# Gradient of x in column strips for 12 of 16 row tiles: where its turns go on SyncE's queue, and five smaller moves

## The chip, the cores and the metric

The kernel runs on one core of one Trainium2 chip. The metric is the device time of one execution in microseconds (us); "the time" is the median over runs. An engine is named as in the profile: PE is TensorE's matmuls, PEld its weight loads, DVE is VectorE, ACT is ScalarE, POOL is GpSimd, SP is SyncE, which here only issues transfers.

## The reference

Forward and backward pass of one block, 2,048 rows (S) by 640 columns (D), in bf16. Only what matters here:

```python
h  = x + attn(layernorm(x), wqkv, wo)          # linear attention, 32 heads of 20
h2 = h + silu(hn @ w1) * (hn @ w3) @ w2        # hn = layernorm(h), F = 1728
# outputs: h2, and by vjp the gradients of x, wqkv, wo, w1, w3, w2
```

The gradient of x ends as: gxn = gq @ Wq.T + gk @ Wk.T + gv' @ W', a contraction over 15 blocks of 128 (five each of q, k and the third, whose rows the kernel keeps as `pkT` with a folded weight). Then the backward layernorm of each row of gxn (two sums over the row, then scale and shift), then the addition of the gradient that comes around the block.

## The kernel before

The rows are 16 tiles of 128 (ST = 16), also seen as 4 chunks of 512 (SC = 4, TPC = 4 tiles each); D is 5 blocks of 128 (DT = 5). Instructions stand on each engine in the order in which the program issues them, by hand; no scheduler moves them. `dma` and `dmaT` (copy, and copy with transposition) go to SP's queue, `dmaG` to POOL's.

The stages follow each other in time: projections and the linear attention (0 to 97 us), the gated MLP forward with half of its backward (97 to 340), gradient of w2 (340 to 398), gradient of hn and of the attention output (398 to 543), then the part that the change touches:

- **Fifth stage** (560 to 611 us): gradients of the q part of wqkv (`wq_jobs((0,))`), the 25 "squares" (L1378), and g_kT, the k gradient in column form (L1439 matmuls, L1445 on DVE). Squares put their result into slots of the ring `obs` (L1452), from where POOL's queue stores it (L1455). `bd`, which served as `gkvT` until then, is free behind that.
- **gxn stage** (611 to 676 us, loop at L1504 and after): `e_gxn(t)` makes the 128 rows of tile t: two halves of 320 columns, 15 matmuls each (L1495), the stationary operand being a 128x128 piece of the turned gradient, the moving one `wqT` with 320 columns. The q piece comes from `e_T(t)` (L1425), which turns g_q's tile t into a slot of `bd`, five tiles ahead. `ln_bwd` follows: ACT takes the row sum while it empties PSUM (L1143), DVE makes the second sum and the combination (L1146 to L1151), ACT scales (L1155), DVE adds (L1156), and SP stores the tile (`out1S`, L1513).
- **Turns of g_k** (`k_turn`, L1487): 20 transfers that bring g_kT back to rows, two per tile, for the k jobs that come next.
- **k jobs** (676 to 698 us): ten weight-gradient jobs of 16 matmuls of 320 columns (L1344), each emptied by ACT (L1348) and stored by SP (L1350). `njob` PSUM banks go round.
- **Last stage** (698 to 815 us): gradients of w1 and w3, 35 jobs of 16 matmuls of 496 columns, with `hnN` (normalised rows of h, loaded over g_q in four parts, L1483) stationary and `gb` blocks (turned from DRAM, L1475) moving. Block 0 of `gb` is loaded in three parts during the last gxn tiles.

Earlier, in the first 97 us, `r_head(t)` scales tile t of the attention's q side and turns it (`r_T`, L385); `r_store` (L735) stores it on POOL's queue. [...]

Of the kernel before, what the change touches and what calls it, by code (L numbers as in the profile page):

```python
# [9 lines left out]
P = 128  # L10
# [45 lines left out]
def kernel(  # L56
# [246 lines left out]
    def phi_rest(keep=0):  # L303
        while len(held) > keep:
            held.pop(0)()
# [78 lines left out]
    def r_T(t):  # L384
        dmaT(out=pqT[:, :, t * P:(t + 1) * P], in_=pqs[t])  # L385
# [47 lines left out]
    def m_end(m, js=(0, 1)):  # L433
        mb = mbs[:, m % 4, :]
        acc = macc[m]
        for j in js:
            A.copy(out=mb[:, j * HD:(j + 1) * HD], in_=acc[j][:, 0:HD])
        if m < 2:
            A.copy(out=Z[:, m:m + 1], in_=acc[1][:, HD:HD + 1])
            z_diag(m)  # L440
        if m < DT - 1:
            dmaT(out=mT[:, :, m * P:(m + 1) * P], in_=mb)
# [134 lines left out]
    def r_row(t):  # L577
        r_red(t)
        r_inv(t)
        r_scale(t)  # L580

    def r_head(t):
        r_row(t)
        r_T(t)
# [24 lines left out]
    phi_rest()  # L609
    m_part(3, range(5))  # L610
    q_tile(6)
    r_head(1)
    r_prod(3)
    phi_rest()
    m_part(3, range(5, 11))
# [4 lines left out]
    phi_rest()  # L620
    m_part(3, range(11, ST))
    m_end(3)
    r_T(2)
    load_w2T(4 * P, 8 * P)
    dmaG(out=m_v[:, 1:4, :], in_=mbs[:, 1:4, :])
# [4 lines left out]
    kvT_block(1, big())  # L630
    r_row(4)
    r_prod(6)
    phi_rest()
    m_part(4, range(5, 11))
    q_tile(9)
# [308 lines left out]
    def kv3():  # L944
# [5 lines left out]
        (f2_wT, 4), (phi_rest,), (q_late, 14), (r_T, 4), (r_head, 5), (load_x, 4, 6), (r_prod, 7),  # L950
        (q_out, 10, 14), (mlp_ghh, 4),
        (q_late, 15), (w2_room,), (sig_table,), (f2_half, 0, 0), (f2_half, 1, 0), (f2_half, 2, 0), (f2_half, 3, 0), (mlp_ghh, 5),
        (f2_half, 0, 1), (r_store, 4, 5), (f2_half, 1, 1), (f2_hn, 0), (r_store, 5, 6), (f2_half, 2, 1), (f2_hn, 1),
        (f2_half, 3, 1), (f2_m_out,),
        (f2_half, 4, 0, True), (mlp_ghh, 6), (f2_half, 4, 1, True), (f2_half, 5, 0, True), (r_red, 6, (0,)), (f2_hn, 2), (f2_hn, 3),
        (f2_ht, 2), (f2_ht, 3), (load_w2T, 8 * P, 10 * P), (mlp_ghh, 7), (r_red, 6, (1,)), (r_inv, 6), (r_scale, 6),
        (r_T, 6), (f2_rest,), (r_red, 7), (r_inv, 7), (r_scale, 7), (r_T, 7), (r_store, 6, 7))
# [177 lines left out]
                    yield  # L1135
        b_ln(acc, t)

    def ln_bwd(acc, t, nrm, st, out, res, pl, gs=None, y=None):

        if gs is None:  # L1140
            gs = pl.tile([P, D], BF16, name="gs", bufs=2)
        s = pl.tile([P, 4], F32, name="s", bufs=2)
        A.activation(out=gs[:].rearrange("p (j n) -> p j n", j=2), in_=acc[:, :, 0:HD], func=AF.Identity,  # L1143
                     accum_out=s[:, 0:1])
        wb = pl.tile([P, D], F32, name="wb", bufs=2)
        V.scalar_tensor_tensor(out=wb[:], in0=gs[:], scalar=1.0, in1=nrm, op0=ALU.mult, op1=ALU.mult,  # L1146
                               accum_out=s[:, 1:2])
        V.tensor_scalar(out=s[:, 2:3], in0=s[:, 1:2], scalar1=-1.0 / D, scalar2=None, op0=ALU.mult)
        V.tensor_scalar(out=s[:, 3:4], in0=s[:, 0:1], scalar1=-1.0 / D, scalar2=st.rs[:, t:t + 1],
                        op0=ALU.mult, op1=ALU.mult)  # L1150
        V.scalar_tensor_tensor(out=wb[:], in0=nrm, scalar=s[:, 2:3], in1=gs[:], op0=ALU.mult, op1=ALU.add)  # L1151

        def rest():
            yt = pl.tile([P, D], BF16, name="y") if y is None else y
            A.activation(out=yt[:], in_=wb[:], func=AF.Identity, bias=s[:, 3:4], scale=st.rs[:, t:t + 1])  # L1155
            V.tensor_tensor(out=out, in0=yt[:], in1=res, op=ALU.add)  # L1156
        return rest
# [176 lines left out]
    def grad_job(lhs, m, rhs, n, out, q=dma):  # L1334
        for _ in grad_halves(lhs, m, rhs, n, out, q):
            pass

    def grad_halves(lhs, m, rhs, n, out, q=dma):

        acc = ps.tile([P, 512], F32, name="job", bufs=njob)  # L1340
        for t in range(ST):
            if t == ST // 2:
                yield
            T.matmul(acc[:, 0:n], lhsT=lhs[:, t, m * P:(m + 1) * P], rhs=rhs(t), start=(t == 0),  # L1344
                     stop=(t == ST - 1))
        ob = obs[:, cnt[0] % (OB // n) * n:(cnt[0] % (OB // n) + 1) * n]
        cnt[0] += 1
        A.copy(out=ob, in_=acc[:, 0:n])  # L1348
        for x, y, to in out:
            q(out=to, in_=ob[:, x:y])  # L1350

    def half(src, j):
        return lambda t: src[:, t, j * HD:(j + 1) * HD]
# [3 lines left out]
    def wq_jobs(ks):  # L1357
        for m in range(DT):
            for k in ks:
                for j in range(2):  # L1360
                    yield from grad_halves(xnN, m, half(gqkv[k], j), HD,
                                           [(0, HD, out2S[:, m, k * D + j * HD:k * D + (j + 1) * HD])],
                                           dma if k else dmaG)
                    yield
# [55 lines left out]

    gT = {}

    def e_T(t):
        gT[t] = bd[:, t % DT, :].rearrange("p (k q) -> p k q", q=P)
        dmaT(out=gT[t], in_=g_q[:, t, :])  # L1425

    mN = U1.tile([P, DT, D], BF16, name="mN", tag="W6")
    load_pkT(2)
# [5 lines left out]
    for n in range(0, SC * DT, 2):  # L1434
        pair = [divmod(i, DT) for i in (n, n + 1)]
        acc = d_acc()
        for b, (c, d) in enumerate(pair):
            for k in range(DT):
                T.matmul(acc[:, b, :], lhsT=gm[:, k, d * P:(d + 1) * P], rhs=xnT[c][:, k, :], start=(k == 0),  # L1439
                         stop=(k == DT - 1))  # L1440
        for b, (c, d) in enumerate(pair):
            cs = slice(c * W, (c + 1) * W)
            pm = dx.tile([P, W], BF16, name="pm", bufs=2)
            V.tensor_scalar(out=pm[:], in0=pkT[:, d, cs], scalar1=1.0, scalar2=None, op0=ALU.min)
            V.scalar_tensor_tensor(out=g_kT[:, d, cs], in0=acc[:, b, :], scalar=gz[:, d:d + 1], in1=pm[:], op0=ALU.add,  # L1445
                                   op1=ALU.mult)
        if n < 16:
            fill(1)
        if 8 <= n < 8 + 2 * DT:
            i = n // 2 - 4  # L1450
            sq = square(mN, gkv_b, i)
            k = (4, 0, 1, 2, 3)[i]  # L1452
            ob = obs[:, k * D:(k + 1) * D]
            unload(sq, ob)
            dmaG(out=out2S[:, i, 2 * D:3 * D], in_=ob)  # L1455
    for t in range(DT):
        e_T(t)
    for _ in jobs:
        pass
    dx.release()  # L1460
    ba.release()


    ex = pool("ex", "right")
    hnN = g_q
    blocks = [(f0, min(f0 + NB, 2 * F)) for f0 in range(0, 2 * F, NB)]
    NB0 = 160

# [11 lines left out]
                for lo, out in ((0, out4S), (F, out5S)) if max(f0, lo) < min(f1, lo + F)]  # L1480

    def load_hnN(i):
        dma(out=hnN[:, i * TPC:(i + 1) * TPC, :], in_=hn_v[:, i * TPC:(i + 1) * TPC, :])  # L1483

    def k_turn(n):
        c, d = divmod(n, DT)
        dmaT(out=g_k[:, c * TPC:(c + 1) * TPC, d * P:(d + 1) * P], in_=g_kT[:, d, c * W:(c + 1) * W])  # L1487

    def e_gxn(t):
        acc = ps.tile([P, 2, 512], F32, name="gxn", tag="gxn", bufs=2)  # L1490
        for j in range(2):
            for k in range(15):
                ts = slice(t * P, (t + 1) * P)
                g = gT[t][:, k, :] if k < DT else g_kT[:, k - DT, ts] if k < 2 * DT else pkT[:, k - 2 * DT, ts]
                T.matmul(acc[:, j, 0:HD], lhsT=g, rhs=wqT[:, k, j * HD:(j + 1) * HD], start=(k == 0),  # L1495
                         stop=(k == 14))
        gx = scr[:, t % 2, :]
        ln_bwd(acc, t, xnN[:, t, :], ln1, gx, g_h[:, t, :], ex, scr[:, 2 + t % 2, :], scr[:, 4, :])()
        return gx

    ps.release()
    ps = pool("pep", space=PSUM)
    njob = 2
    jobs = wq_jobs((1,))  # L1504
    scr = U1.tile([P, DT, D], BF16, name="scr", tag="W6")
    for t in range(ST):
        gx = e_gxn(t)
        if t + DT < ST:
            e_T(t + DT)
        for n in (2 * t, 2 * t + 1):  # L1510
            if n < SC * DT:
                k_turn(n)
        dma(out=out1S[:, t, :], in_=gx)  # L1513
        if t > 10 and t < 15:
            load_hnN(t - 11)
        if t in (11, 13, 15):
            load_block(0, (t - 11) // 2 * NB0, (t - 9) // 2 * NB0 if t < 15 else NB)
    load_block(1)
    for _ in jobs:
        pass  # L1520
# [20 lines left out]
    for i, (f0, f1) in enumerate(blocks):  # L1541
        n = f1 - f0
        for m in range(DT):
            last = (i, m) == (len(blocks) - 1, DT - 1)
            for a, b in ((0, n - P), (n - P, n)) if last else ((0, n),):
                c = (a + b) // 2
                halves = ((a, c), (c, b)) if i * DT + m < 6 else ((a, b),)
                out = [(x + y - a, z + y - a, to) for y, w in halves for x, z, to in both_grads(m, f0 + y, f0 + w)]
                grad_job(hnN, m, lambda t: gb[i][:, t, a:b], b - a, out, A.dma_start)
        load_block(i + 2)  # L1550
        if 0 < i <= 4:
            gw2_out(i - 1)
        if i < 4:
            gw2_turn(i)
# [37 lines left out]
```

## Time and profile before

| what | value |
|---|---|
| time, 3 runs | median 821.31 us (820.56 to 822.07) |
| the profiled execution | 819.31 us, of which the span is 817.3 us |
| PE | 812.6 us busy, 5,227 matmuls and as many weight loads |
| DVE, ACT, POOL | 444.9, 324.4 and 128.6 us busy |
| gxn stage, 611 to 676.2 us | PE 65.2 us (no gap), DVE 37.3, ACT 25.7, DMA engines 62% |
| k jobs, 676.2 to 698 us | PE 21.8 us (no gap), DMA engines 114% by the view's count |
| granted clock of PE | 1.00 in every stage |

The page gives busy time per engine, a strip of 40 slices, the chain of work that ended last, and groups of instructions by line. Other views used below: the chain in order of time, the timeline of one engine, busy time by stage, and the transfers of a stretch of time. In the timeline of SP's queue an entry's length is how long SP was held by issuing the transfer; its landing is counted separately, from issue to the last byte.

### The profile page before, as it was taken

Reading aid. Unit: us, or ns where it says so; the run is one execution under the profiler, and the core shown is the slowest. Engines: PE = TensorE matmul, PEld = TensorE weight load, DVE = VectorE, ACT = ScalarE, POOL = GpSimd, SP = SyncE. Lnnn points to the kernel's source line nnn. Section 1 sums busy time; section 2 is a strip of 40 time slices with the busy share of each in tenths; the row PEclk is TensorE's granted clock in tenths of the full one; section 3 lists DMA queues with packets and bytes.
Section 4 is the critical chain, followed back from the end, with each engine's and each line's share of the span. In section 5 each row is a group of like instructions: output and inputs, shape, how many; then the busy total and the mean of one; then the engine's idle time right before and its main releaser. Section 6 shows DMA issues by size and latency. Waiting matters only on the chain.

```text
span 817.3 us, 13571 instructions
## 1 busy us (share of the span) xinstructions
PE 812.6 (99%) x5227; PEld 495.2 (61%) x5227; DVE 444.9 (54%) x976; ACT 324.4 (40%) x607; POOL 128.6 (16%) x194
## 2 busy tenths in 40 slices
PE   9999999999999999999999999999999999999998
PEld 6777544555555555754577777777657777544444
DVE  7859997998898566300057777772565551000000
ACT  7856688665565666011122212222113442111111
POOL 2243333323222212100001111110120000000000
PEclk9999999999999999999999999999999999999999
DMA  9799899696485556999867887259995679679991
GB/s 257 210 241 283 207 264 317 203 243 175 125 211 154 169 173 168 227 263 239 242 176 182 211 198 199 58 114 180 214 184 104 122 166 255 177 179 233 239 220 38
DMA packets 334480, 159.83 MB, mean 196 GB/s; under 512 B 252304, under 2 KB 327920, under 8 KB 334416
## 3 DMA queue, kind: packets, MB, share of 16 engines
q1 hardware_dynamic: 290976, 119.37, 62.7%
q0 software_dynamic: 7008, 23.17, 8.4%
q10 hardware_dynamic: 36432, 16.42, 8.2%
q8 instruction: 41, 0.67, 0.3%
q14 instruction: 23, 0.19, 0.1%
HBM read 44.47 MB, written 53.43 MB: 120 GB/s over the span
## 4 chain that ended last, share of the span: by engine, by line
PE 98%; DVE 1%; ACT 0%; DMA 0%; POOL 0%; issue 0%
PE mm L395 21%; PE job L1344 20%; PE ghn L1131 14%; PE gxn L1495 8%; PE gw L1086 7%; PE big L268 4%; PE o L913 4%; PE o L859 3%; PE gwo L1219 3%; PE macc L430 3%; PE at L657 3%; PE gr L1188 3%; PE dkv L1439 3%; PE mm L268 1%; PE dkv L1378 1%; PE gp L395 1%
## 5 line engine op out<-in xcount | busy, mean ns | idle before, releaser
L1344 PE MATMUL job<-gb,g_q 128*128 128x496 bf16 (+3 forms) x576 | 116.8, 366 | 0.0
L1131 PEld LDWEIGHTS <-ggb 128*128 128x128 bf16 x864 | 84.5, 98 | 33.0
L395 PE MATMUL mm<-pqT,w 128*128 128x512 bf16 x405 | 93.6, 379 | 0.0
L1344 PEld LDWEIGHTS <-g_q 128*128 128x128 bf16 x576 | 55.8, 98 | 61.0
L395 PEld LDWEIGHTS <-w 128*128 128x128 bf16 x540 | 52.6, 98 | 63.0 <-issue 0.8
L1348 ACT CAST obs<-job 128x496 bf16<-128x496 f32 (+4 forms) x56 | 28.6, 511 | 136.5 <-PE job L1344 126.0
L1131 PE MATMUL ghn<-w13a,ggb 128*128 128x320 bf16 x448 | 63.5, 299 | 0.0
L1131 PE MATMUL ghn<-w13b,ggb 128*128 128x320 bf16 x416 | 61.4, 299 | 0.0
L1146 DVE SCALAR_TENSOR_TENSOR wb<-gs,hnb 128x640 f32<-128x640 bf16 x16 | 13.2, 825 | 88.1 <-ACT gs L1143 88.1
L395 PE MATMUL mm<-g2T,w2T 128*128 128x512 bf16 x240 | 59.6, 379 | 0.0
L1086 PE MATMUL gw<-hb,g 128*128 128x512 bf16 (+2 forms) x320 | 58.6, 346 | 0.0
L1086 PEld LDWEIGHTS <-g 128*128 128x128 bf16 x320 | 31.3, 98 | 26.9
L420 ACT CAST ghh<-mm 128x512 bf16<-128x512 f32 x48 | 28.1, 585 | 47.6 <-PE mm L395 41.2
L1196 POOL TENSOR_TENSOR sz<-Zb,g_h 128x640 f32<-128x640 bf16 x16 | 20.2, 1261 | 163.6 <-DVE g_h L1197 163.6
L796 ACT ACTIVATE sig<-mm 128x512 bf16<-128x512 f32 x56 | 33.7, 602 | 25.2 <-PE mm L395 21.7
L1143 ACT ACTIVATE gs<-ghn 128x640 bf16<-128x640 f32 x16 | 11.2, 703 | 77.1 <-PE ghn L1131 77.1
L395 PEld LDWEIGHTS <-w2T 128*128 128x128 bf16 x260 | 25.4, 98 | 23.4
L268 PEld LDWEIGHTS <-pqT 128*128 128x128 bf16 x320 | 30.7, 98 | 13.5 <-ACT pqT L260 0.9
L1344 PEld LDWEIGHTS <-g 128*128 128x128 bf16 x320 | 31.0, 98 | 12.8
L268 PE MATMUL big<-wqkv,pqT 128*128 128x320 bf16 x250 | 38.5, 299 | 0.2
L832 DVE TENSOR_TENSOR gate<-gate,sig 128x1024 bf16<-128x1024 bf16 x28 | 19.3, 689 | 33.8 <-ACT gate L807 31.1
L1091 ACT CAST gw2o<-gw 128x512 bf16<-128x512 f32 (+2 forms) x20 | 10.4, 519 | 65.5 <-PE gw L1086 25.5
(212 smaller groups left out, 1378.1 us busy)
## 6 DMA issues: line engine op xcount, KB each, us to landing
hh_d<-hhT SPq DMA_DIRECT2D x24, 256.0 KB, 2.8
gg_d<-gate POOLq DMA_DIRECT2D x24, 256.0 KB, 4.4
gg_d<-ghh POOLq DMA_DIRECT2D x24, 256.0 KB, 4.1
ggb<-gg_d SPq DMA_DIRECT2D x6, 896.0 KB, 5.4
ggb<-gg_d ACTq DMA_DIRECT2D x6, 832.0 KB, 5.6
ggb<-gg_d SPq DMA_DIRECT2D x2, 1728.0 KB, 12.6
x_sb<-in_A_x_dram SPq DMA_DIRECT2D x4, 640.0 KB, 5.1
pk_d<-pk_all SPq DMA_DIRECT2D x4, 640.0 KB, 5.7
```

The source lines that it names most:

```text
L268: T.matmul(acc, lhsT=pqT[:, c, t * P:(t + 1) * P], rhs=wqkv[:, c, n0:n0 + HD], start=(c == 0), stop=(c == DT - 1))
L395: T.matmul(acc[:], lhsT=w[:, c, fc * P:(fc + 1) * P], rhs=rhs[:, c, :], start=(c == 0), stop=(c == DT - 1))
L420: A.copy(out=ghh[n // 2][:, n % 2, :], in_=acc[:])
L430: T.matmul(macc[m][j][:, 0:n], lhsT=pk_all[:, t, m * P:(m + 1) * P], rhs=x_ext[:, t, j * HD:j * HD + n], start=(t == 0), stop=(t == ST - 1))
L657: T.matmul(at[:, 0:HD], lhsT=pqT[:, c, t * P:(t + 1) * P], rhs=Wp[:, c, j * HD:(j + 1) * HD], start=(c == 0 and not on_pe), stop=(c == DT ...
L796: A.activation(sig[:, i, :], gp[:], AF.Sigmoid)
L913: T.matmul(o2["ps"][:, 0:HD], lhsT=hhT[c][:, fc, i * P:(i + 1) * P], rhs=w2[:, fc, j * HD:(j + 1) * HD], start=(fc == 0), stop=(fc == FT - 1))
L1086: T.matmul(acc[:, 0:fw], lhsT=g2[:, t, m * P:(m + 1) * P], rhs=hb[b][:, t, 0:fw], start=(t == 0), stop=(t == ST - 1))
L1131: T.matmul(acc[:, j, 0:HD], lhsT=ggb[t // 2][:, k, lo:lo + P], rhs=rhs[:, j * HD:(j + 1) * HD], start=(k == 0), stop=(k == NG - 1))
L1344: T.matmul(acc[:, 0:n], lhsT=lhs[:, t, m * P:(m + 1) * P], rhs=rhs(t), start=(t == 0), stop=(t == ST - 1))
L1348: A.copy(out=ob, in_=acc[:, 0:n])
L1495: T.matmul(acc[:, j, 0:HD], lhsT=g, rhs=wqT[:, k, j * HD:(j + 1) * HD], start=(k == 0), stop=(k == 14))
```

## The change

The gradient of x is made in transposed form for chunks 0 to 2. `e_gxT(c, ds)` swaps the operands: a 128x128 piece of `wqT` is stationary, and 512 columns (the rows of the chunk) of the turned gradients move. It makes strips of 128 columns by 512 rows, two per PSUM buffer (5 per chunk); ACT copies each strip to one of three `gxT` buffers, and SP turns it back into rows, which land in g_q's own rows (free by then). The layernorm then works from those rows, with its first sum on DVE (`reduce_sum`), one chunk behind PE. The last four tiles keep the old form, with rows written to g_q by ACT.

With that: `e_T(c)` turns a chunk, into `bd` for chunks 0 and 2 and into `obs` for 1 and 3, two chunks ahead. Eight `k_turn`s go ahead of the stage and the other twelve between strips. The stores of gradient of x go to POOL's queue. `hnN`'s last four tiles are loaded into `bd`, as g_q's last rows are still in use; the second half of each layernorm (`rest`) is held back by one tile; the k jobs get four PSUM banks and the last four layernorms go between them. `load_block(1)` is issued after those. The squares use slots 0 to 3 of `obs` (the fifth slot 0 again). In the first 97 us, the turn of tile 1 goes behind that of `mT`'s block 3, the store of tile 4 goes right behind the products of tile 6, and that of tile 5 goes behind the store of m. The first seven (not six) jobs of the last stage store in halves.

Cut to its core:

```diff
-    r_head(1)
+    r_row(1)
...
     m_end(3)
+    r_T(1)
     r_T(2)
...
+    dmaG(out=r_v[:, 4, :], in_=pqs[4])
...
-        (f2_half, 0, 1), (r_store, 4, 5), (f2_half, 1, 1), (f2_hn, 0), (r_store, 5, 6), (f2_half, 2, 1), (f2_hn, 1),
-        (f2_half, 3, 1), (f2_m_out,),
+        (f2_half, 0, 1), (f2_half, 1, 1), (f2_hn, 0), (f2_half, 2, 1), (f2_hn, 1),
+        (f2_half, 3, 1), (f2_m_out,), (r_store, 5, 6),
...
-            k = (4, 0, 1, 2, 3)[i]
+            k = i % 4
...
-    def e_T(t):
-        gT[t] = bd[:, t % DT, :].rearrange("p (k q) -> p k q", q=P)
-        dmaT(out=gT[t], in_=g_q[:, t, :])
+    def e_T(c):
+        gT[c] = (obs[:] if c % 2 else bd[:].rearrange("p k n -> p (k n)"))[:, 0:DT * W].rearrange("p (k w) -> p k w", w=W)
+        for i in range(TPC):
+            dmaT(out=gT[c][:, :, i * P:(i + 1) * P], in_=g_q[:, c * TPC + i, :])
...
-    for t in range(DT):
-        e_T(t)
+    e_T(0)
+    k_turn(8)
     for _ in jobs:
         pass
+    e_T(1)
...
+    def e_gxT(c, ds):
+        acc = ps.tile([P, 2, 512], F32, name="gxn", tag="gxn", bufs=2)
+        for b, d in enumerate(ds):
+            for k in range(15):
+                T.matmul(acc[:, b, :], lhsT=wqT[:, k, d * P:(d + 1) * P], rhs=gx_src(c, k, 0, W), start=(k == 0),
+                         stop=(k == 14))
+        for b, d in enumerate(ds):
+            gxT = ex.tile([P, W], BF16, name="gxT", bufs=3)
+            A.copy(out=gxT[:], in_=acc[:, b, :])
+            dmaT(out=g_q[:, c * TPC:(c + 1) * TPC, d * P:(d + 1) * P], in_=gxT[:])
...
+    def e_ln(*ts):
+        for t in ts:
+            rest = ln_bwd(None, t, xnN[:, t, :], ln1, scr[:, t % 2, :], g_h[:, t, :], ex, g_q[:, t, :], scr[:, 4, :],
+                          sums.get(t))
+            e_rest()
+            ends.append((t, rest))
...
-    njob = 2
+    njob = 4
...
-    for t in range(ST):
-        gx = e_gxn(t)
-        if t + DT < ST:
-            e_T(t + DT)
-        for n in (2 * t, 2 * t + 1):
-            if n < SC * DT:
-                k_turn(n)
-        dma(out=out1S[:, t, :], in_=gx)
-        if t > 10 and t < 15:
-            load_hnN(t - 11)
-        if t in (11, 13, 15):
-            load_block(0, (t - 11) // 2 * NB0, (t - 9) // 2 * NB0 if t < 15 else NB)
+    for c in range(SC - 1):
+        for n, ds in enumerate(((0, 1), (2, 3), (4,))):
+            e_gxT(c, ds)
+            if c > 0:
+                e_ln(*((c - 1) * TPC + i for i in ((0,), (1, 2), (3,))[n]))
+            k_turn(((2, 2, 0), (0, 1, 0), (2, 2, 0))[c][n])
+        if c + 2 < SC:
+            e_T(c + 2)
+        if c == 1:
+            load_hnN(0)
+    for i in range(TPC):
+        t = ST - TPC + i
+        e_gxn(t)
+        e_ln(t - TPC)
+        if i == 0:
+            k_turn(3)
+            load_hnN(1)
+        else:
+            load_block(0, (i - 1) * NB0, i * NB0 if i < 3 else NB)
+    fill(1)
+    load_hnN(3)
+    e_ln(ST - TPC)
+    load_hnN(2)
+    for i in range(1, TPC):
+        fill(2)
+        e_ln(ST - TPC + i)
+    e_rest()
     load_block(1)
...
-                halves = ((a, c), (c, b)) if i * DT + m < 6 else ((a, b),)
+                halves = ((a, c), (c, b)) if i * DT + m < 7 else ((a, b),)
```

`e_rest` runs the held second half (ACT scale, DVE add) and stores the tile on POOL's queue; `fill(n)` issues n half jobs.

More of the change, by code (lines that the diff above doesn't have):

```diff
@@ L1136, in b_ghn, with ln_sum, ln_bwd @@
         b_ln(acc, t)
[L1138 to L1143, printed above, removed]
-                     accum_out=s[:, 0:1])
+    def ln_sum(acc, gs, s):
+        A.activation(out=gs.rearrange("p (j n) -> p j n", j=2), in_=acc[:, :, 0:HD], func=AF.Identity,
+                     accum_out=s[:, 0:1])
+    def ln_bwd(acc, t, nrm, st, out, res, pl, gs=None, y=None, s=None):
+        if acc is not None:
+            gs = pl.tile([P, D], BF16, name="gs", bufs=2)[:]
+        if s is None:
+            s = pl.tile([P, 4], F32, name="s", bufs=2)
+            if acc is not None:
+                ln_sum(acc, gs, s)
+            else:
+                V.reduce_sum(out=s[:, 0:1], in_=gs, axis=AX.X)
         wb = pl.tile([P, D], F32, name="wb", bufs=2)
-        V.scalar_tensor_tensor(out=wb[:], in0=gs[:], scalar=1.0, in1=nrm, op0=ALU.mult, op1=ALU.mult,
+        V.scalar_tensor_tensor(out=wb[:], in0=gs, scalar=1.0, in1=nrm, op0=ALU.mult, op1=ALU.mult,
                                accum_out=s[:, 1:2])
@@ L1150, in ln_bwd @@
                         op0=ALU.mult, op1=ALU.mult)
-        V.scalar_tensor_tensor(out=wb[:], in0=nrm, scalar=s[:, 2:3], in1=gs[:], op0=ALU.mult, op1=ALU.add)
+        V.scalar_tensor_tensor(out=wb[:], in0=nrm, scalar=s[:, 2:3], in1=gs, op0=ALU.mult, op1=ALU.add)
         def rest():
@@ L1343, in grad_halves @@
                 yield
-            T.matmul(acc[:, 0:n], lhsT=lhs[:, t, m * P:(m + 1) * P], rhs=rhs(t), start=(t == 0),
+            T.matmul(acc[:, 0:n], lhsT=lhs(t)[:, m * P:(m + 1) * P], rhs=rhs(t), start=(t == 0),
                      stop=(t == ST - 1))
@@ L1360, in wq_jobs @@
                 for j in range(2):
-                    yield from grad_halves(xnN, m, half(gqkv[k], j), HD,
+                    yield from grad_halves(lambda t: xnN[:, t, :], m, half(gqkv[k], j), HD,
                                            [(0, HD, out2S[:, m, k * D + j * HD:k * D + (j + 1) * HD])],
@@ L1421, with k_turn @@
     gT = {}
-    def e_T(t):
-        gT[t] = bd[:, t % DT, :].rearrange("p (k q) -> p k q", q=P)
-        dmaT(out=gT[t], in_=g_q[:, t, :])
+    def e_T(c):
+        gT[c] = (obs[:] if c % 2 else bd[:].rearrange("p k n -> p (k n)"))[:, 0:DT * W].rearrange("p (k w) -> p k w", w=W)
+        for i in range(TPC):
+            dmaT(out=gT[c][:, :, i * P:(i + 1) * P], in_=g_q[:, c * TPC + i, :])
+    turns = iter(range(SC * DT))
+    def k_turn(n):
+        for _ in range(n):
+            c, d = divmod(next(turns), DT)
+            dmaT(out=g_k[:, c * TPC:(c + 1) * TPC, d * P:(d + 1) * P], in_=g_kT[:, d, c * W:(c + 1) * W])
     mN = U1.tile([P, DT, D], BF16, name="mN", tag="W6")
@@ L1464 @@
     ex = pool("ex", "right")
-    hnN = g_q
     blocks = [(f0, min(f0 + NB, 2 * F)) for f0 in range(0, 2 * F, NB)]
@@ L1482, in load_hnN, with hn_row, gx_src @@
     def load_hnN(i):
[L1483 to L1487, printed above, removed]
+        to = g_q[:, i * TPC:(i + 1) * TPC, :] if i < SC - 1 else bd[:, 0:TPC, :]
+        dma(out=to, in_=hn_v[:, i * TPC:(i + 1) * TPC, :])
+    def hn_row(t):
+        return g_q[:, t, :] if t < ST - TPC else bd[:, t - ST + TPC, :]
+    ends, sums = [], {}
+    def gx_src(c, k, a, b):
+        src = (gT[c], g_kT, pkT)[k // DT]
+        off = 0 if k < DT else c * W
+        return src[:, k % DT, off + a:off + b]
+    def e_gxT(c, ds):
[8 more added lines that the diff above has]
+            dmaT(out=g_q[:, c * TPC:(c + 1) * TPC, d * P:(d + 1) * P], in_=gxT[:])
     def e_gxn(t):
+        c, i = divmod(t, TPC)
         acc = ps.tile([P, 2, 512], F32, name="gxn", tag="gxn", bufs=2)
@@ L1492, in e_gxn @@
             for k in range(15):
[L1493 to L1499, printed above, removed]
+                T.matmul(acc[:, j, 0:HD], lhsT=gx_src(c, k, i * P, (i + 1) * P), rhs=wqT[:, k, j * HD:(j + 1) * HD],
+                         start=(k == 0), stop=(k == 14))
@@ new lines, in e_gxn, with e_rest @@
+        sums[t] = ex.tile([P, 4], F32, name="sr", bufs=TPC)
+        ln_sum(acc, g_q[:, t, :], sums[t])
+    def e_rest():
+        while ends:
+            t, rest = ends.pop()
+            rest()
+            dmaG(out=out1S[:, t, :], in_=scr[:, t % 2, :])
+    def e_ln(*ts):
[4 more added lines that the diff above has]
+            ends.append((t, rest))
@@ L1518 @@
+    for i in range(TPC):
[5 more added lines that the diff above has]
+            load_hnN(1)
+        else:
+            load_block(0, (i - 1) * NB0, i * NB0 if i < 3 else NB)
[7 more added lines that the diff above has]
+    e_rest()
     load_block(1)
@@ L1546 @@
                 c = (a + b) // 2
-                halves = ((a, c), (c, b)) if i * DT + m < 6 else ((a, b),)
+                halves = ((a, c), (c, b)) if i * DT + m < 7 else ((a, b),)
                 out = [(x + y - a, z + y - a, to) for y, w in halves for x, z, to in both_grads(m, f0 + y, f0 + w)]
-                grad_job(hnN, m, lambda t: gb[i][:, t, a:b], b - a, out, A.dma_start)
+                grad_job(hn_row, m, lambda t: gb[i][:, t, a:b], b - a, out, A.dma_start)
         load_block(i + 2)
```

## The prediction

> **What bounds the kernel.** I read the page's head and first part, then the chain in order of time, then the gxn stage by engine.
>
> The page: PE is busy for all but 4.7 us of the span, and the chain that ended last is PE's own.
>
> ```profile
> span 817.3 us, 13571 instructions
> PE 812.6 (99%) x5227; PEld 495.2 (61%) x5227; DVE 444.9 (54%) x976; ACT 324.4 (40%) x607; POOL 128.6 (16%) x194
> ...
> PE 98%; DVE 1%; ACT 0%; DMA 0%; POOL 0%; issue 0%
> ```
>
> The chain in time (start, length, what): from 606 us to the end there is no other engine in it. The gxn stage is 480 matmuls in 65.20 us, 135.8 ns each at 320 columns; the matmuls of 512 columns just ahead take 2.16 us for ten, in the trace 215.8 ns each.
>
> ```profile
> 606.36 2.16 PE dkv L1439 x10
> 608.85 2.16 PE dkv L1439 x10
> 611.00 65.20 PE gxn L1495 x480
> 676.21 138.39 PE job L1344 x736
> ```
>
> So a change here wins only PE time, and it loses whatever makes PE wait. What could make PE wait is SP's queue. Its timeline (start, length, what) shows one turn after the other, each holding the queue:
>
> ```profile
> 644.80 2.56 SPq L1487 DMA_TRANSPOSE g_k<-g_kT  x2
> 647.46 0.52 SPq L1513 DMA_DIRECT2D out_dram<-scr  x1
> 648.08 2.56 SPq L1425 DMA_TRANSPOSE bd<-g_q  x1
> 650.69 2.57 SPq L1487 DMA_TRANSPOSE g_k<-g_kT  x2
> 653.36 0.53 SPq L1513 DMA_DIRECT2D out_dram<-scr  x1
> 653.98 1.20 SPq L1425 DMA_TRANSPOSE bd<-g_q  x1
> ```
>
> A g_k turn costs the queue 1.31 us with the gap behind it, a g_q turn 1.25 (653.98 to the next at 655.23). They land about 1.25 us after that. The turn at 648.08 took 2.56 us: 1.35 us more. In the stretch 646 to 651 us the list of DMA queues has one packet that is none of the kernel's data:
>
> ```profile
> q1 hardware_dynamic: 1734, 0.56, 83.8%
> q8 instruction: 1, 0.02, 2.2%
> ```
>
> The trace has such packets at 613.3, 631.2, 648.5 and 665.6 us, every 17.4 us on average (128 pairs of weight load and matmul at 135.8 ns). Around them SP lost 0.2 us (613), 0.8 (631) and 1.35 (648).
>
> **PE's work.** 12 of 16 tiles lose 360 matmuls of 320 columns (360 x 135.83 ns = 48.90 us) and get 3 x 5 x 15 = 225 of 512 columns (225 x 215.8 ns = 48.56 us). Gain **0.34 us**, from 135 matmuls fewer. The order of instructions confirms the 135. The weight loads (98 ns) lie beneath either length. [...]
>
> **Turns: does PE wait?** SP's queue is unchanged up to the first g_q turn at 601.59. Before, the fifth began at 607.29, so four take until then. Then, by the rows above: eight g_k turns (8 x 1.31) to 617.8, four g_q turns for chunk 1 (4 x 1.25) to 622.8, strips 0 and 1 of chunk 0 to 625.4, two g_k turns to 628.0, strips 2 and 3 to 630.6, two g_k turns to 633.3, strip 4 to 634.6, four g_q turns for chunk 2 to 639.6, strip 0 of chunk 1 to 640.9. A strip's turn was never run; it has the form of a g_k turn (128x512 in, 4 blocks out), so 1.31. Bounds: 1.25, and 1.70, the longest spacing under traffic (604.23 to 605.93).
> PE begins chunk 0 at 610.84 (timeline), and each chunk is 75 x 215.8 ns = 16.19 us: chunk 1 at 627.03, chunk 2 at 643.21. What they need:
> - Chunk 1's buffer held strips 2 and 3 of chunk 0. Strip 3's copy (ACT, 0.59 us by the row of ghh casts, L420) takes the `gxT` of strip 0, free when that turn lands at 624.1 + 1.25 = 625.3. Copy done at 626.0: **1.0 us early**.
> - Chunk 2's buffer held strips 2 and 3 of chunk 1, and strip 3's copy needs the turn of that chunk's strip 0, landing at 640.9 + 1.25 = 642.1. Copy done at 642.8: **0.4 us early**.
> - Chunk 2's own g_q turns land at 640.9: 2.3 us early. Chunk 1's at 624.0: 3 us early.
>
> Nothing is late at bare prices, but 0.4 us is less than one instruction packet costs. PE's instructions come at 215.8 ns a pair now, so those packets come every 128 x 215.8 = 27.6 us: about 614.7 and 642.3. The first falls among the eight g_k turns (0.2 to 1.35 us lost, middle 0.8), the second on the landing that chunk 2 waits for (0 to 1.35). Lateness 0.2 to 2.7 less 0.4 of slack: 0 to 2.3 us of wait. I take **0.8**, near one packet's middle cost plus half of a second, less the slack. The queue behind that first wait (strips, chunk 3's g_q turns, `hnN` and `gb` loads) has 3 us and more: chunk 3's turns land at 653.7 and PE needs them at 659.4.
>
> **Layernorms.** The added row sum on DVE has no row of this shape; 2 x 320 elements cost 0.87 us (L374), a plain pass of 640 in bf16 0.49 (L1156). I take 0.8. A tile is then 0.8 + 1.9 + 0.5 = 3.2 us (rows below) against 4.05 us of PE per tile, so DVE keeps up, but it starts a chunk behind.
>
> ```profile
> 620.02 0.83 DVE L1146 SCALAR_TENSOR_TENSOR wb<-scr,g 128x640 f32<-128x640 bf16 x1 [0.65 <-ACT scr L1143]
> ...
> 621.08 0.88 DVE L1151 SCALAR_TENSOR_TENSOR wb<-g,s,scr 128x640 f32<-128x640 bf16 x1
> 623.01 0.49 DVE L1156 TENSOR_TENSOR scr<-scr,g_h 128x640 bf16<-128x640 bf16 x1 [1.05 <-ACT scr L1155]
> ```
>
> The queue continued at these prices, chunk 2's last strip lands near 666. Four tiles at 3.2 and four without the sum at 2.4 end near 688.5, ACT's last scale (0.92) near 689.4, and the cast of k job 3 stands behind that scale on ACT: 689.8. PE wants its bank for job 7 at 610.84 + 48.56 + 16.30 + 7 x 2.17 = 690.9. So 1.1 us of slack, at no cost. It is gone if the stores, now POOL's, take over some 5.2 us: each DVE add waits for the store of two tiles ahead (`scr` has two slots).
>
> **No cost, with the cover named.** 15 copies for 12 row sums on ACT: 25.7 of 65.2 us busy. Loads for the last stage: `gb` block 0 leaves SP near 686 (before at 687.8) and `hnN`'s last part near 687, landing 5 us later (its row: 5.4); PE needs them at 697.5. `load_block(1)` stands behind three stores that wait for casts 0 to 2 and leaves SP near 696 (before at 695.45), needed at 714. Squares' slots: job 8's cast no longer waits for a store; PE had no gap there. Tile 1's turn held SP for 2.46 us at 67.65 and is needed at 86.5. Tile 4's store finds POOL idle from 74.6 to 84.2; before, it landed at 95.10 and hn's tile 2, in the same buffer, was made at 95.18, but DVE was busy until 95.11 anyway. PE's gap there is 0.27 us: gain 0 to 0.3, I take 0. Halves of a seventh store: 0.35 us of ACT's queue.
>
> **Sum.** 819.31 - 0.34 + 0.8 = 819.8 us against the profiled execution (its 2.0 us outside the span taken as they are). It lies 2.0 us under the median of the three runs (821.31), so the same difference, +0.46 us, gives **821.8 us**. No change means within 0.2% (1.64 us), about what a measurement of this kernel can tell.
>
> **Rivals.**
> - *A, forecast: PE waits 0 to 1.9 us in all, at chunk 2 above all.* 821.0 to 822.9. For: slack 0.4 against packets of 0.2 to 1.35. Chance 0.60.
> - *B, no wait, and the 0.27 us near 96 us goes too.* 821.31 - 0.34 - 0.27 = 820.7, still within 0.2%. For: every step is on time at bare prices. Chance 0.13.
> - *C, slower: the turns follow each other more slowly.* All 30 entries from 601.59 to strip 0 of chunk 1 are turns, with no plain copy between them, and 26 come behind the first four. Each 0.05 us more per turn makes that strip 26 x 0.05 = 1.3 us later. It decides from 0.09 us more on: lateness 2.4, less 0.4 of slack and the 0.34 won, is the bound. At 1.45 in place of 1.31 the wait is 3.2 us and the time 824.2. Against: two in a row and a copy show 1.31 and 1.36 without a growing landing time. Chance 0.13.
> - *D, slower: the last layernorms hold the casts.* Stores of 160 KB from POOL took 3.4 us to land in the middle, one of 80 KB under load 6.5. At 6 us the pair of tiles takes 1.5 us more, so job 7 waits about 2: 821.31 - 0.34 + 0.5 + 2 = 823.5. Against: 8 us of DMA load there are turns for `gb`. [...] Chance 0.09.
> - *E, faster by over 1.64 us:* something that the timed runs have and the profiled one, 2 us shorter, does not (the store that hn's tile 2 waits for). 819.4. Against: after 14 us no single gap of PE in the trace is over 0.3 us. Chance 0.05.
>
> That the strips are not made, or that matmuls stay, is excluded by the order of instructions. Faster 0.05; same 0.60 + 0.13 = 0.73; slower 0.22. The range 820.0 to 824.2 takes A, B with the scatter of the runs (0.75 us), D, and C up to turns of 1.45 us.
>
> **What would show it.** PE in the gxn stage: 225 matmuls at 215.8 ns and 120 at 135.8, 64.86 us. A gap of PE at the first matmul of chunk 2 (near 643), released by ACT's copy and that by a turn: A. Turns spaced at 1.4 and a gap at chunk 1 too: C. A gap among the k jobs released by a cast: D. No gap: B. It is wrong if PE waits for the `gb` or `hnN` loads near 697, or at a place before 560.

## The result, and the profile after

| | kernel before | kernel after |
|---|---|---|
| median | 820.93 us (820.53 to 822.07, 6 runs) | 825.05 us (823.26 to 825.94, 6 runs) |
| the profiled execution | 819.31 us, span 817.3 | 825.89 us, span 824.2 |

The kernel is slower: ratio 1.0049, 95% interval 1.0038 to 1.0060. The prediction was 821.8 us in 820.0 to 824.2; the measured time lies above that range. The two profiled executions lie at opposite ends of their runs (before's under all of its timed ones, after's next to its slowest), so the profiles differ by 6.9 us of span where the medians differ by 4.1.

The page of the kernel after: PE has 135 matmuls fewer, as foreseen, but the chain that ended last is no longer PE's alone.

```profile
span 824.2 us, 13354 instructions
...
PE 814.4 (99%) x5092; PEld 482.8 (59%) x5092; DVE 451.9 (55%) x988; ACT 322.1 (39%) x598; POOL 137.7 (17%) x210
...
PE 90%; DMA 4%; issue 3%; DVE 1%; ACT 1%; POOL 0%; SPq 0%; POOLq 0%; DVEq 0%; ACTq 0%
```

PE's timeline (start, length, what, and in brackets the idle time before it and what ended it) has two long pauses that before did not have:

```profile
661.72 0.84 PE L1529 MATMUL gxn<-wqT,obs 128*128 128x320 bf16 x5 [1.36 <-ACT gxT L1521]
...
696.71 8.13 PE L1353 MATMUL job<-g_k,g 128*128 128x320 bf16 x48 [3.31 <-ACT obs L1357]
```

The first is where the last chunk's rows begin (L1529), the second is the eighth k job. From start to start, less the usual pace, they are 1.52 and 3.48 us; these figures are used below. The 48 matmuls behind the second took 8.13 us; at 135.8 ns they would take 6.5. The granted clock by stretch (stretch, its length, then the busy time and count of PE, PEld, DVE, ACT and POOL, PE's clock, DMA share, GB/s) says why. The first two lines are the kernel before, the last two the kernel after:

```profile
676.00:698.00 22.00, 22.00 (x164) 15.77 (x163) 2.87 (x7) 5.45 (x13) 0.00 (x0) 1.00 1.14 261
698.00:706.00 8.00, 8.00 (x40) 3.77 (x39) 0.00 (x0) 1.54 (x3) 0.00 (x0) 1.00 0.85 192
...
676.00:698.00 22.00, 18.69 (x135) 13.10 (x133) 16.52 (x42) 9.48 (x18) 3.78 (x7) 0.96 1.09 259
698.00:706.00 8.00, 8.00 (x51) 5.20 (x50) 0.49 (x1) 1.27 (x3) 0.54 (x1) 0.89 0.88 225
```

In the trace's clock records it is 0.5 from 696.29 to 699.71, and eleven matmuls there start 267 ns apart in place of 136: 1.45 us in all.

The chain in order of time leads back from both pauses:

```profile
655.48 5.53 DMA g_q<-gxT
...
661.08 0.58 ACT gxT L1521
...
687.50 5.05 DMA out_dram<-scr
...
692.64 0.49 DVE scr L1165
...
696.25 0.41 ACT obs L1357
...
696.71 124.79 PE job L1353 x624
```

*The first pause.* A strip of the last transposed chunk took 5.53 us to come back as rows, where the strips of chunk 0, with no load beside them, took 2.4 to 2.6. Its copy buffer came free late, so ACT copied the chunk's fourth strip late (L1521), and PE waited for the PSUM buffer. SP's queue shows what stood ahead of that turn: a plain load of 640 KB of hn, issued 0.63 us earlier.

```profile
654.85 0.53 SPq L1501 DMA_DIRECT2D g_q<-hn_d  x1
655.48 2.57 SPq L1522 DMA_TRANSPOSE g_q<-gxT  x2
```

*The second pause.* DVE's add (L1165) writes one of two slots that POOL stores from. Its timeline, the adds alone:

```profile
686.71 0.49 DVE L1165 TENSOR_TENSOR scr<-scr,g_h 128x640 bf16<-128x640 bf16 x1 [1.28 <-DMA out_dram<-scr]
...
692.64 0.49 DVE L1165 TENSOR_TENSOR scr<-scr,g_h 128x640 bf16<-128x640 bf16 x1 [1.33 <-DMA out_dram<-scr]
...
699.64 0.49 DVE L1165 TENSOR_TENSOR scr<-scr,g_h 128x640 bf16<-128x640 bf16 x1 [4.25 <-DMA out_dram<-scr]
```

Each waits for the store of two tiles ahead. These adds are 5.9 and 7.0 us apart, two tiles each; DVE's own work for two of these tiles is 2 x 2.26 us. The add releases the only slot for ACT's scaled row, so ACT's next scale waits as well, and the cast that PE wants stands behind it. ACT:

```profile
695.42 0.92 ACT L1164 ACTIVATE scr<-wb,sr,ln_rs 128x640 bf16<-128x640 f32 x1 [1.34 <-DVE scr L1165]
696.25 1.38 ACT L1357 CAST obs<-job 128x320 bf16<-128x320 f32 x4
```

Four casts stood ready behind that scale; PE wanted the first at 693.2. The list of transfers from 674 to 698 us (what, queue, count, size, median us to landing) shows how long the stores took:

```profile
out_dram<-scr POOLq DMA_DIRECT2D x8, 160.0 KB, 5.1
```

The sum from the trace: 1.52 + 3.48 + 1.45, 0.48 at 566 us (a turn that landed late, in code that is unchanged) and some 0.2 more than before near 97 us, less 0.34 for the matmuls: 6.8 of the 6.9 us.

### The profile page after: what moved, and what is told of

Read it like the earlier page. It is cut to its first block, busy times and chain, and to the rows that moved or that the text cites. A ratio compares the mean times of both kernels' runs of the same rounds, so it can differ in the third digit from the quotient of the medians.

```text
span 824.2 us, 13354 instructions
## 1 busy us (share of the span) xinstructions
PE 814.4 (99%) x5092; PEld 482.8 (59%) x5092; DVE 451.9 (55%) x988; ACT 322.1 (39%) x598; POOL 137.7 (17%) x210
## 4 chain that ended last, share of the span: by engine, by line
PE 90%; DMA 4%; issue 3%; DVE 1%; ACT 1%; POOL 0%; SPq 0%; POOLq 0%; DVEq 0%; ACTq 0%
PE mm L395 20%; PE job L1353 17%; PE ghn L1133 14%; PE gw L1088 7%; PE big L268 4%; PE o L915 4%; PE gxn L1517 4%; PE o L861 3%; PE gwo L1228 3%; PE macc L430 3%; PE gr L1197 3%; PE dkv L1456 3%; PE at L659 2%; DMA g_q<-gxT 1%; PE mm L268 1%
## 5 line engine op out<-in xcount | busy, mean ns | idle before, releaser
L1353 PE MATMUL job<-gb,g_q 128*128 128x496 bf16 (+3 forms) x432 | 93.4, 366 | 0.0
L1353 PEld LDWEIGHTS <-g_q 128*128 128x128 bf16 x432 | 41.8, 98 | 45.8
L1517 PEld LDWEIGHTS <-wqT 128*128 128x128 bf16 x225 | 22.0, 98 | 26.6
```

Of the source, the lines that this page charges most:

```text
L1353: T.matmul(acc[:, 0:n], lhsT=lhs(t)[:, m * P:(m + 1) * P], rhs=rhs(t), start=(t == 0), stop=(t == ST - 1))
L1517: T.matmul(acc[:, b, :], lhsT=wqT[:, k, d * P:(d + 1) * P], rhs=gx_src(c, k, 0, W), start=(k == 0), stop=(k == 14))
```

## The experiments

The theories, as the expectations number them. **1**: the two slots, together with stores that land in 5 to 6 us, hold ACT and by it PE. **2**: the hn load ahead of the last strips makes that chunk late, and the tail with it. **3**, which goes with 1: the delay reaches PE only because the casts stand behind the scales on ACT. **4**, a rival: stores from POOL's queue cost as such. Two more rivals are that the small moves cost the time and that the half-speed clock has another cause than the pause.

| kernel | median us | before, same chip | ratio to before, 95% interval |
|---|---|---|---|
| four slots | 820.00 | 820.35 | 0.9994 (0.9984 to 1.0003) |
| hn load later | 824.28 | 820.35 | 1.0056 (1.0038 to 1.0073) |
| both of these | 819.54 | 820.35 | 0.9991 (0.9980 to 1.0002) |
| before, small moves alone | 820.19 | 820.35 | 1.0000 (0.9989 to 1.0011) |
| before, stores on POOL | 820.06 | 820.48 | 0.9997 (0.9986 to 1.0008) |
| stores on SP | 835.41 | 820.48 | 1.0176 (1.0157 to 1.0195) |
| PE kept at work, first try | 824.27 | 820.48 | 1.0046 (1.0031 to 1.0061) |
| casts first | 820.61 | 820.48 | 0.9996 (0.9987 to 1.0005) |
| the kernel after, again | 824.78 | 820.37 | 1.0049 (1.0032 to 1.0066) |
| PE kept at work, second try | 823.08 | 820.37 | 1.0031 (1.0019 to 1.0042) |
| all three edits | 818.82 | 820.37 | 0.9982 (0.9972 to 0.9992) |
| no early gb loads | 821.06 | 820.37 | 1.0007 (0.9996 to 1.0018) |

**Four slots.**

```diff
-            dmaG(out=out1S[:, t, :], in_=scr[:, t % 2, :])
+            dmaG(out=out1S[:, t, :], in_=scr[:, t % 4, :])
...
-    rest = ln_bwd(..., scr[:, t % 2, :], ...)
+    rest = ln_bwd(..., scr[:, t % 4, :], ...)
```

> The kernel after, with four slots in turn for the layernorm's sums and their stores in place of two; nothing else. Theory 1 (the tail waits for slots): VectorE's add for row tile 14 no longer waits for the landing of tile 12's store, ScalarE's scales and the third cast come about 2 us earlier, and TensorE's wait before the eighth k job falls from 3.48 us to at most 1.1; with so short a wait the granted clock stays at full speed there, which gives back 1.45 us more. The wait of 1.5 us at the start of the gxn matmuls of the last chunk stays. Sum: 3.8 us off 825.1, some 821.2 to 822.0. Theory 2 (the late start of the last chunk alone makes the layernorms late): the wait in the tail stays at 2.5 us or more and the time within 1 us of 825.1. Theory 4 (the stores on GpSimd's queue cost as such, by slowing the turns and loads beside them): the wait moves by less than 0.5 us and the time is 824.5 to 825.5.

The whole loss is gone, more than expected: 1.0049 - 0.9994 of 820 us is 4.5 us, and 820.00 lies under the 821.2 to 822.0 of theory 1. The chain in time of its profiled execution (the slowest of its ten runs) shows the k jobs with a pause of 0.2 us in place of 3.48, while a pause of 2.1 us at the last chunk is still there (how much of it the nine faster runs have, no trace shows):

```profile
663.51 16.46 PE gxn L1529 x120
679.97 15.21 PE job L1353 x112
...
695.22 123.33 PE job L1353 x624
```

Its stores land no sooner (median 5.9 us from 674 to 698); only nobody waits for them.

**The hn load later.**

```diff
-        if c == 1:
-            load_hnN(0)
...
             k_turn(3)
+            load_hnN(0)
             load_hnN(1)
```

> The kernel after, with the load of the first hn block put behind the strips of the last chunk and the fourth k turn on SyncE's queue, beside the second block's load; two slots stay. Theory 2 (the load ahead of the strips makes the last chunk late): the first strip of the last chunk is issued some 0.6 us earlier and lands in 2.5 to 3.5 us in place of 5.5, the wait of 1.52 us at its first gxn matmul goes, its last strip lands some 4 us earlier (667 in place of 671), the layernorms of the last tiles start that much earlier, and the wait before the eighth k job falls to 1.2 us or less with the granted clock at full speed: 820.0 to 821.5. Theory 1 alone (slots): the 1.5 us goes, while the tail's 3.5 us wait and the half-speed stretch behind it stay, 823 to 824. Theory 4 (the stores beside the strips are what slows them): the first strip still lands after 660.5, less than 0.5 us is gained, 824.5 to 825.5.

Half of theory 2 holds: the first strip now lands 3.2 us after its issue (657.88), and the pause at the last chunk is gone. The other half falls. PE comes to the k jobs sooner and waits there the longer, until the same moment as before (697.12 against 696.71):

```profile
690.56 2.33 PE L1353 MATMUL job<-g_k,g 128*128 128x320 bf16 x16 [0.62 <-ACT obs L1357]
697.12 8.35 PE L1353 MATMUL job<-g_k,g 128*128 128x320 bf16 x48 [4.23 <-ACT obs L1357]
```

So the pause of 1.5 us cost nothing in the kernel after: the later one would have taken it. The last strip landed at 669.22, 2.1 us sooner than in the kernel after and 2.2 later than expected, but the stores then took longer (median 6.0 us from 674 to 698), and the adds waited for them.

**Both.**

> Both edits at once: four slots, and the first hn block's load behind the last chunk's strips. Theories 1 and 2 together: no wait over 0.5 us in the gxn stage or between the k jobs, no stretch of half speed, and what is left against the kernel before is the matmuls' saving of 0.34 us against the small waits at 97.8 and 566: 820.3 to 821.3, within 0.2% of the kernel before. If the stores on GpSimd's queue cost as such: 823 or more, with waits for landings left in the chain.

819.54 us, below the expected band, with no pause over 0.35 us behind the first 13 us of its profile. Against four slots alone the gain is 0.5 us, which the intervals don't separate.

**The small moves alone**, made to the kernel before: `r_row(1)` and `r_T(1)`, the two `r_store` moves, `k = i % 4`, and 7 in place of 6 halved jobs.

> The kernel before, with the four small moves alone (the squares' output slots, the turned row block's place, the two stores' places, the halves of the first products that the changed kernel splits) and without the turned gradient. Theories 1 and 2: these cost at most the 0.2 us that the first MLP matmul waits longer at 97.8, so 820.5 to 821.4, no difference from the kernel before that can be measured. Rival (the small moves cost what was lost): 823 to 825.

No difference: this rival falls.

**Stores on POOL in the kernel before.**

```diff
-        dma(out=out1S[:, t, :], in_=gx)
+        dmaG(out=out1S[:, t, :], in_=gx)
```

> The kernel before, its gradient by rows as it was and its slots as they were, with the stores of x's gradient put on GpSimd's queue in place of SyncE's. Theory 1 (the cost is the return of two slots, not the queue): VectorE has no two-slot turn here, so nothing waits for the landings, and the time stays within 1 us of the kernel before, 819.5 to 821.3. Theory 4 (stores that GpSimd issues cost as such, by slowing the turns and loads beside them): 823 or more, with TensorE waiting for ScalarE's copies or casts in the last stages.

No difference, so theory 4 falls; but the expectation is wrong in saying that the kernel before has no two-slot turn. It has one, with the same `scr[:, t % 2]`. Its tiles come at PE's pace of 4.07 us, and a slot is wanted again after 8.1 us. From 660 to 684 us its POOL stores land as late as those of the kernel after, one after 7.1 us, and nothing waits for them:

```profile
out_dram<-scr POOLq DMA_DIRECT2D x6, 160.0 KB, 5.8
```

**Stores on SP in the kernel after.**

```diff
-            dmaG(out=out1S[:, t, :], in_=scr[:, t % 2, :])
+            dma(out=out1S[:, t, :], in_=scr[:, t % 2, :])
```

> The kernel after with two slots, its stores of x's gradient on SyncE's queue in place of GpSimd's. If the long landings come from the traffic they share (the loads and turns of the same stretch) and not from the queue that issues them, the stores still land in 4 to 8 us in the tail and the wait before the eighth k job stays, 3 us or more; besides, SyncE now stands at each store until VectorE's add is done, and the turns and loads behind it come later: 825 to 832. If GpSimd's queue is what makes them long, they land in about 2.5 us, the add waits no more, and the time is 820.5 to 822.

Slower still, by more than expected. From SP the stores land in 2.0 us (median) between 640 and 674, and beside the loads of the tail in

```profile
out_dram<-scr SPq DMA_DIRECT2D x6, 160.0 KB, 4.4
```

So the loads make them long, not the queue: POOL's took 5.1 us there (median) in the kernel after. SP, standing at each store until the add is done, brings the rest late: PE pauses of 2.1, 2.2, 1.1 and 6.0 us.

**PE kept at work.** Between the seventh and the eighth k job:

```diff
+    fill(7)
+    warm = ps.tile([P, 2, 512], F32, name="gxn", tag="gxn", bufs=2)
+    for _ in range(12):
+        T.matmul(warm[:, 0, :], lhsT=ones[:], rhs=wqT[:, 0, 0:512], start=True, stop=True, skip_group_check=True)
```

> The kernel after with twelve more matmuls of 512 columns (2.6 us of work whose result nobody uses) between the seventh and the eighth k job, where TensorE stands for 3.48 us. If the half-speed stretch behind that wait comes from the idle time, TensorE's granted clock stays at 1.0 from 690 to 706, the eleven matmuls at 267 ns take 136, and the time is 1.45 us less than the kernel after: some 823.1 to 824.0 at the pace of this chip. If the clock falls for another reason, the stretch at half speed stays and the time is that of the kernel after or up to 0.5 us more: 824.3 to 825.5.

The profile shows what the first theory of the clock says: the extra matmuls fill 2.75 us of the pause (PE sits idle for 1.24 behind them), the eighth job starts at the same time as in the kernel after (696.57), and its 48 matmuls take 6.68 us in place of 8.13. The granted clock is 1.00 throughout.

```profile
692.57 2.75 PE L1583 MATMUL gxn<-wqT,ones 128*128 128x512 bf16 x12
696.57 6.68 PE L1353 MATMUL job<-g_k,g 128*128 128x320 bf16 x48 [1.24 <-ACT obs L1357]
```

The median, 1.0046 of before, does not separate from that of the kernel after. So both ran once more, on one chip:

> The kernel after once more, so that it runs beside the next kernel on one chip, with as many timed runs: 1.0049 times the kernel before or within 0.0015 of that, some 824.0 to 825.3, with a wait of 3 to 4.5 us before the eighth k job and some 3.4 us at half speed behind it.

> The twelve extra matmuls (nobody uses their result) between the seventh and the eighth k job, now beside the kernel after on the same chip: the first try showed no half speed in its profile and yet a median only 0.3 us below. If the half-speed stretch costs every run its 1.45 us, this is 1.0 to 1.7 us below the kernel after run beside it. If the extra matmuls are paid for elsewhere or most unprofiled runs keep their clock, it is within 0.5 us of it.

The kernel after repeats its 1.0049, and the second try lies 1.70 us under it. The 1.45 us is shown by the rows of the profiles; in the times it was 0.3 (by the ratios) and 1.7 us in two tries, and their intervals overlap those of the kernel after.

The mean granted clock of each run says more. A stretch of 3.41 us at half speed lowers the mean of a run of 824 us to 0.998. Of the twelve runs of the kernel after, nine have 0.998 (median 825.11 us) and three 1.000 (median 823.31); all sixteen runs with the extra matmuls have 1.000. So the stretch comes in most runs, not in all, and the extra matmuls take it away. The runs without it are 1.8 us shorter, but no trace shows how long PE's pause was in them.

**Casts first**, with two slots and the old place of the hn load; `load_block(1)` goes ahead of the last layernorm:

```diff
-    for i in range(1, TPC):
-        fill(2)
-        e_ln(ST - TPC + i)
-    e_rest()
+    fill(3)
+    e_ln(ST - 3)
+    fill(4)
+    e_ln(ST - 2)
     load_block(1)
+    fill(4)
+    e_ln(ST - 1)
+    fill(4)
+    e_rest()
```

> The kernel after with its two slots; in the tail the casts for the coming k jobs are written ahead of the last layernorms' scales on ScalarE, instead of between them. The adds go on waiting for the stores' landings and the last layernorm ends as late or later, but no cast stands behind it. If the wait reached TensorE only by the order on ScalarE, the wait of 3.48 us before the eighth k job and the half-speed stretch go and the time is 820.0 to 821.5 (the 1.5 us at the last chunk's gradient stays in some runs). If the casts wait for something else (the loads of the gradient's turned blocks), the wait stays above 2 us and the time above 823.

The loss is gone this way too. The adds wait as long as ever:

```profile
692.49 0.49 DVE L1165 TENSOR_TENSOR scr<-scr,g_h 128x640 bf16<-128x640 bf16 x1 [2.39 <-DMA out_dram<-scr]
697.36 0.49 DVE L1165 TENSOR_TENSOR scr<-scr,g_h 128x640 bf16<-128x640 bf16 x1 [2.52 <-DMA out_dram<-scr]
```

and the last one is even later (700.63), but PE has no pause in the 160 matmuls of the k jobs:

```profile
678.10 21.90 PE L1353 MATMUL job<-g_k,g 128*128 128x320 bf16 x160
```

Theory 3 holds: the stores' wait costs only through the casts behind it.

**No early gb loads.**

```diff
+    gb[0] = ex.tile([P, ST, NB], BF16, name="gb", bufs=2)
+    nc.gpsimd.memset(gb[0][:], 0)
     for c in range(SC - 1):
...
-            load_block(0, (i - 1) * NB0, i * NB0 if i < 3 else NB)
+            pass
```

> The kernel after with two slots and the old order, whose three early loads of the first turned gradient block are replaced by GpSimd writing zeros ahead of the stage (the gradients that use this block are zero). If the stores land late because of the loads beside them, the stores of the tail land in 2.3 to 4 us except beside the loads of hn, VectorE's adds wait less than 1 us in all for them, the wait before the eighth k job falls to 1 us or less with no half-speed stretch, and the time is 820.0 to 822.0. If the stores in quick succession slow each other, they go on landing in 5 to 6 us, and the wait stays above 2.5 us and the time above 823.5.

Three stores that have little or no load beside them (one the last 1.2 us of an hn load, one the first 0.7 us of `load_block(1)`) land in 2.05 to 2.07 us, those beside hn's loads in 3.4 to 4.6, and two that lie wholly beside `load_block(1)` in 5.6 and 6.8. The median of the tail falls from 5.1 to 3.8 us, and PE's pause from 3.48 to 0.59:

```profile
695.01 6.68 PE L1353 MATMUL job<-g_k,g 128*128 128x320 bf16 x48 [0.43 <-ACT obs L1357]
```

So the length of the stores comes from the loads, with two slots a cost and with four none. (Without gb's loads one of the hn loads is issued 10 us earlier, so the two kinds are not fully taken apart.)

**All three edits**: four slots, the hn load later, the casts first.

> The kernel after with four slots, the first hn block's load behind the last chunk's strips, and the casts ahead of the last layernorms. With each of the first and the third alone the loss was gone, so nothing is left to gain in the tail over either; what the second gives is the wait of 1 to 2 us at the last chunk's gradient. Sum: 819.3 to 820.5, 0 to 1 us below the kernel before, ratio 0.9985 to 1.0.

This version beats both kernels, by a little more than expected: 818.82 us, 1.5 us under the kernel before, the ratio's interval clear of 1. In its chain the matmuls of the stage and the k jobs run through without a pause:

```profile
659.61 16.30 PE gxn L1529 x120
675.91 138.39 PE job L1353 x736
```

The stage runs from 611.04 to 675.91, 64.87 us. Before it was 65.20: the 0.33 us is the gain in matmuls. Profile against profile it is 0.6 us faster (818.68 against 819.31): 0.30 us within the span (816.97 against 817.27), which is the matmuls' gain, and 0.33 outside it. Outside the span lie 2.0 us in the runs of the kernel before (median) and 1.7 in these, as in those of the kernel before with its stores on POOL; why is open. Why the medians differ by 0.9 us more isn't settled either: its runs scatter less than those of the kernel before, and before has one profile only.

## Why the prediction was wrong

- **PE's work** was right: 64.86 us for the gxn matmuls predicted, 64.87 measured once nothing holds them. (That no other engine stands in the chain to the end leaves out its last 2.7 us, a cast and a store behind PE; they are the same in both kernels.)
- **Turns, the wait at chunk 2** (+0.8) was right in kind. The 25 turns from 606.13 to 640.83 us took 2.4 us more than priced: 1.3 beside the instruction packet of 615.08 (one turn held SP 2.58 us), 0.7 near 633, and 0.5 because four g_q turns in a row took 5.26 us, not 5.0. The next such packet came at 645.41, not near 642.3, and so behind the landing (643.26) that chunk 2 needed. So in the profile of the kernel after the copy is just on time, and this wait is 0. In three of the other ten profiles with strips PE waits 0.6 to 1.3 us at 645 to 646, and with four slots the chain leads from there through ACT's copy and a turn to SP's queue. Rival C, turns that are all slower, falls: away from other traffic they follow each other at 1.24 to 1.37 us.
- **"The queue behind that first wait ... has 3 us and more"** failed. The reckoning gave a strip its quiet 2.5 us. Behind an hn load and beside a POOL store it took 5.5, and PE waited 1.5 us; without that load ahead of it 3.2. In the sum of the kernel after this counts for nothing, as the experiment with the later load shows.
- **Layernorms: "So 1.1 us of slack, at no cost"** is the step that failed and made the error: PE waited 3.48 us there. DVE's price was right (2.98 and 2.26 us per tile measured, 3.2 and 2.4 taken). Two other terms were not. Chunk 2's last strip landed at 671.36, not near 666. By the tiles' measured prices the cast would then have ended near 693.7 (an estimate), half a microsecond after PE wanted it: PE was late itself, 693.2 in place of 690.9. That used the slack up. What made the wait is the landing of the stores. The text named the threshold, some 5.2 us, and named what follows (rival D), but held it for unlikely at 0.09. Seven of the eight stores issued from 674 to 698 us took 4.7 to 6.5 us. The nearest rows of before were not read for it: SP's own stores beside the same loads, issued at 673.24 and 681.08, landed after 4.65 and 6.43 us. The list of transfers around each shows them:

```profile
out_dram<-scr SPq DMA_DIRECT2D x1, 160.0 KB, 4.7
...
out_dram<-scr SPq DMA_DIRECT2D x1, 160.0 KB, 6.4
```

They harmed nothing there, because a slot was wanted again only after 8.1 us. The change halved that time to about 4.5 in the last four tiles, and this, not the queue, was the thing to price.

- **Rival D was right as a mechanism and too small**: 2 us of wait foreseen, 3.48 in the profile. The delay goes round: the add at 686.71 was 1.28 us late for want of a slot, its own store (687.50) landed at 692.55, and the add after the next was late by another 1.33. And the 1.1 us of slack in front of them was gone with the late strip.
- **The clock was missing from every case.** The pause of 3.48 us brought a stretch at half speed that cost another 1.45: the clock records have 3.41 us at 0.5 there (696.29 to 699.71), and 1.00 with the extra matmuls in the pause.
- **"No cost, with the cover named"** held: the small moves cost nothing, and PE did not wait for `gb` or `hnN` near 697.
- **POOL's stores beside DVE's work** show no delay of their own: in the kernel after each holds POOL 0.54 us, and the one issued at 663.31, with DVE at work, landed in 2.3 us. Without the early gb loads they landed in 2.05 to 2.07 us where little or no load was in flight; SP's took 2.0 (median, stores on SP, 640 to 674).

## What to carry to other kernels

When work that was spread over a stage at PE's pace is moved into a burst, ask first how soon each buffer slot is wanted again (here after 8.1 us before and about 4.5 after), and price the transfer that frees it by its rows under the traffic of its new place (4.7 to 6.5 us for seven of eight stores). A wait on an engine off the bound cost nothing here until something the bound needs stood behind it in the same queue: with the casts first, DVE's adds waited 2.39 and 2.52 us and PE did not pause. So put that ahead, or give the buffer more slots. And price a pause of PE with a possible stretch at half speed behind it: in these profiles pauses of 1.5 and 2.1 us brought none, one of 2.2 us and one of 3.48 us did, the last at a cost of 1.45 us.

## What was not expected of the hardware

- The clock fell after pauses of PE of quite different length. In the kernel after, one of 1.52 us was followed by no fall and one of 3.48 us went with 3.41 us at 0.5. With the stores on SP, a pause of 2.2 us (its end at 691.84) was followed by 3.41 us at 0.5, and one of 6.0 us (its end at 704.89) went with 6.83 us; with four slots one of 2.1 us (its end at 663.51) was followed by none.
- The lengths of the clock records agree with one step of 3.413 us: the records at full clock that end in a fall last 689.49, 692.91 and 686.08 us in the kernel after, with the hn load later and with the stores on SP, which is 202, 203 and 201 steps; the stretches at 0.5 are one step (3.41) and two (6.83). Whether a pause's place in these steps counts beside its length, and whether three runs of the kernel after kept their clock by it, is not shown.
- Stores of 160 KB took more than twice as long beside the loads of `hn` and `gb`, from either queue: from SP 2.0 us (median) before the tail and 4.4 beside its loads (stores on SP); from POOL 2.05 to 2.07 with hardly a load in flight (three stores, no early gb loads) and 5.1 (median) beside the loads (the kernel after).
